# Gaps of 64 bytes between the parts of an SBUF arena, in a chunked-attention, MLP and Strassen mixture kernel

## The chip, the cores and the metric

The kernel runs on one core of a Trainium2 chip. The metric is the device time of one execution in microseconds (us), the median of several runs.

## What is computed

The reference chains three pieces. Its inputs are float32.

```python
# attention within chunks of 64 positions: q, k, v are (4, 8, 576, 64)
scores = scale * matmul(q_c, k_c.T);  attn = exp(scores - max);  attn /= attn.sum + 1e-9
x = (attn @ v_c), heads side by side                       # 2304 x 512
# MLP: w_in 512 x 2048, w_out 2048 x 512
h = maximum(x @ w_in, 0);  x = h * h @ w_out
# mixture of 4 experts, w1 512 x 1024, w2 1024 x 512 each
p = domain_probs / (domain_probs.sum(-1) + 1e-9)
out = sum over e of p[:, e] * (maximum(x @ w1[e], 0) @ w2[e])
```

## The kernel before

Every large product is done three times in float32r: both operands are split into a high and a low part (ACT copies the high part, DVE or POOL subtract it), and high x high, high x low and low x high are summed in PSUM. So a product of a weight tile with a moving tile is three matmuls, each with its own load of 128 x 128 weights. A load runs on the second track of TensorE (PEld in the profile) beside the matmul before it.

All float32r operands but one stand in one SBUF tile, the **arena** `ar` (128 partitions x 128 KiB). Its parts are cut out by hand, by offsets in float32 elements, and it is used twice with two layouts:

- Attention and MLP. `x`, high and low, in five blocks of 384 or 512 tokens (`new_x`); a ring of converted MLP weights (`RING_AT`, `unit_split`); two pairs of buffers for the squared hidden layer (`GP_AT`, in `l1`). `l1` (matmul at L300) multiplies weights from the ring by a block of `x`, `l2` (L333) weights from the ring by a hidden buffer. Each does 12 matmuls, then the other takes its turn.
- Mixture. Seven slots of combined inputs `Y` (`y_slot`), two sets of hidden parts (`S_AT`), two slots of first-layer weights (`W1_AT`, high and low side by side), and one slot of second-layer weights (`W2_AT`); the other second-layer slot is a tile of its own, `w2x`. The loop over `n` (48 steps: 3 super-blocks of tokens x 4 experts x 4 pairs of hidden tiles) has seven units `u`. In each, `c_unit` (L596) does 6 matmuls of 384 columns, with weights from `W1_AT[n % 2]` and one `Y` slot as the moving operand: the first layer as a Strassen-like product of seven. Between these blocks stand second-layer matmuls of the step before: `plain_unit` for steps 0 to 10 (L708, blocks of 6 with 512 columns) and `d_unit` for steps 11 to 47 (L691, blocks of 9 with 256 columns, again seven products). There the hidden parts `g` are the weights, and the split second-layer weights the moving operand: from `W2_AT` where `n` is even, from `w2x` where `n` is odd.

The order on each engine is written out by hand (`tc.manual_schedule()`), with tables for the second layer. DMAs go through SP's queue. During the first 20 ticks attention is interleaved: per tick `s1_stage` has DVE take a maximum (`mx`, L241) and subtract it (L242) twice, and `norm_stage` on DVE sums (`sm`, L253), adds, inverts and scales the tile before. `mx` and `sm` are small tiles, two buffers each.

In front of the change every part of the arena starts at a multiple of 512 bytes from the arena's start, and each 128-column slice of float32 is 512 bytes long. So weights and moving operand, where both are in the arena, stand a multiple of 512 bytes apart. `w2x` starts 155,840 bytes behind the arena's start, which is 304 x 512 + 192.

Of the kernel before, what the change touches and what calls it, by code (L numbers as in the profile page):

```python
# [10 lines left out]
F32 = mybir.dt.float32  # L11
# [7 lines left out]
P = 128  # L19
CH = 64  # L20
BLOCKS = [384, 384, 512, 512, 512]
# [9 lines left out]
RAW_BUFS = 4  # L31
CV_BUFS = 4
HALF = 384
NSUP = 3
LAG_A = 2
UOFF = [1, 3, 5, 16, 8, 17, 18, 19]
# [10 lines left out]
def tile_kernel(ctx, tc, q, k, v, moe_w_in, moe_w_out, moe2_p, moe2_w1, moe2_w2, out):  # L47
    nc = tc.nc
    B, H, S, D = q.shape
# [3 lines left out]
    KD = DM // P  # L53
    HX = H // 2
# [6 lines left out]
    NB = len(BLOCKS)  # L61
    starts = [sum(BLOCKS[:i]) for i in range(NB)]
# [13 lines left out]
    qkp = att.enter_context(tc.tile_pool(name="qkp", bufs=2, side="right"))  # L76
# [1 line left out]


    XW = 2 * KD * NT  # L80
    RING_AT = XW
    GP_AT = RING_AT + RING * 4 * DM
    AR = GP_AT + (LAG + 1) * 2 * 512
    ar = arena.tile([P, AR], F32R, name="ar")


    NY, NW, NS7 = 14 * 2 * HALF, 7 * 2 * P, 14 * HALF
    Y_AT = 0
    S_AT = [NY, NY + NS7]
    W1_AT = [GP_AT - 2 * NW, NY + 2 * NS7]  # L90
    W2_AT = [W1_AT[1] + 2 * NW, GP_AT]
    assert W2_AT[0] + NW <= W1_AT[0] and W2_AT[1] + NW <= AR
    assert W1_AT[0] >= RING_AT + (RING - 2) * 4 * DM

# [3 lines left out]
    def bank(tags):  # L98
        n = turn.get(tags, 0)
        turn[tags] = n + 1  # L100
        tag = tags[n % len(tags)]
        return ps.tile([P, 512], F32, tag=tag, name="ps" + tag, bufs=BUFS[tag])
# [46 lines left out]
    def unit_split(n, which):  # L149
        a = cv.pop((n, which))  # L150
        o = RING_AT + (n % RING * 4 + 2 * which) * DM
        h, l = ar[:, o:o + DM], ar[:, o + DM:o + 2 * DM]
# [14 lines left out]
    qT, kT, et, aT = {}, {}, {}, {}  # L167

    def new_x(tb):
        o, w = 2 * KD * starts[tb], KD * BLOCKS[tb]  # L170
        xh[tb] = ar[:, o:o + w].rearrange("p (k t) -> p k t", k=KD)
        xl[tb] = ar[:, o + w:o + 2 * w].rearrange("p (k t) -> p k t", k=KD)

# [53 lines left out]
    def s1_stage(t, tags):  # L227
        qt, kt = qT.pop(t), kT.pop(t)
        pt = [bank(tags)[:, :HX * CH].rearrange("p (j k) -> p j k", j=HX) for _ in range(2)]
        for c in range(2):  # L230
            cs = slice(c * CH, (c + 1) * CH)
            for j in range(HX):
                for x in range(2):
                    r = slice(x * CH, (x + 1) * CH)
                    nc.tensor.matmul(  # L235
                        pt[x][cs, j, :], lhsT=qt[r, j, cs], rhs=kt[r, j, cs], start=True, stop=True
                    )
        e = qkp.tile([P, HX, 2, CH], F32, tag="e", name="e", bufs=LAG_A + 1)
        mx = qkp.tile([P, 2, HX, 1], F32, tag="mx", name="mx")
        for x in range(2):  # L240
            nc.vector.tensor_reduce(out=mx[:, x], in_=pt[x], axis=AX.X, op=ALU.max)  # L241
            nc.vector.tensor_tensor(  # L242
                out=e[:, :, x, :], in0=pt[x], in1=mx[:, x].to_broadcast([P, HX, CH]), op=ALU.subtract
            )
        et[t] = e
# [3 lines left out]

    def norm_stage(t):  # L250
        e = et[t].rearrange("p j x k -> p (j x) k")
        sm = qkp.tile([P, H, 1], F32, tag="sm", name="sm")
        nc.vector.tensor_reduce(out=sm, in_=e, axis=AX.X, op=ALU.add)  # L253
        nc.vector.tensor_scalar_add(sm, sm, 1e-9)
        nc.vector.reciprocal(sm, sm)
        nc.vector.tensor_tensor(out=e, in0=e, in1=sm.to_broadcast([P, H, CH]), op=ALU.mult)
# [106 lines left out]
    NP = nf2 // 2  # L363
    NQ = NSUP * E * NP
    rows = {}
    for sp in range(NSUP):
        if sp < NSUP - 1:
            r = [starts[2 * sp] + i * P for i in range(3)] + [starts[2 * sp + 1] + i * P for i in range(3)]
        else:
            r = [starts[NB - 1] + i * P for i in range(3)] + [starts[2 + i] + HALF for i in range(3)]  # L370
        rows[sp] = r
# [4 lines left out]
    comb = {}  # L376

    def y_slot(i):
        o = Y_AT + i * 4 * HALF
        return [ar[:, o + z * 2 * HALF:o + (z + 1) * 2 * HALF].rearrange("p (k t) -> p k t", k=2) for z in range(2)]  # L380

    def y_half(a, k):
        return a[:, 2 * k:2 * k + 2, :HALF]

# [3 lines left out]
    def y_blocks(sp):  # L388
        if sp < NSUP - 1:
            return acc[2 * sp], acc[2 * sp + 1]  # L390
        return acc[NB - 1], acc[0]

    def y_combine(sp):

        a, b = y_blocks(sp)
        y11, y21, y12, y22 = y_half(a, 0), y_half(a, 1), y_half(b, 0), y_half(b, 1)
        c = comb[sp] = {Y11: y11, Y21: y21, Y22: y22}
        if sp == 0:
            t1, t2, t3, t4 = y11, y22, y12, y21
        else:  # L400
            u, w = (acc[0], acc[1]) if sp == 1 else (acc[1], acc[2])
            t1, t2, t3, t4 = y_half(u, 0), y_half(u, 1), y_half(w, 0), y_half(w, 1)
        if sp == 0:
            for i in (Y11, Y21, Y22):
                yield from y_split(sp, i)
        sub(t1, y12, y11)
        yield
        sub(t3, y22, y12)
        yield
        sub(t2, y22, t1)  # L410
        yield
        sub(t4, y21, t2)
        c.update({T1: t1, T2: t2, T3: t3, T4: t4})
        yield
        if sp == 0:
            for i in (T1, T2, T3, T4):
                yield from y_split(sp, i)

    def y_split(sp, i):
        h, l = y_slot(i)  # L420
        a = comb[sp][i]
        nc.scalar.copy(h, a)
        eng = nc.vector if sp == 0 or i in (Y11, Y21, Y22) else nc.gpsimd
        eng.tensor_tensor(out=l, in0=a, in1=h.bitcast(F32), op=ALU.subtract)
        yield

    def y_gather():

        for i in range(3):
            nc.gpsimd.tensor_scalar(  # L430
                out=acc[0][:, :, i * P:(i + 1) * P], in0=acc[2 + i][:, :, HALF:], scalar1=1.0,
                scalar2=None, op0=ALU.mult,
            )
            yield
# [73 lines left out]
    def w1_slot(n):  # L508
        o = W1_AT[n % 2]
        w1c[n] = ar[:, o:o + NW], ar[:, o + NW:o + 2 * NW]  # L510
        return ar[:, o:o + 2 * NW].bitcast(F32)
# [36 lines left out]

    def w2_split(n, part):
        if part == 0:  # L550
            o = S_AT[n % 2] + 8 * HALF
            w2c[n] = [ar[:, o + z * 2 * DM:o + (z + 1) * 2 * DM].rearrange("p (h d) -> p h d", h=2) for z in range(2)]
        h, l = (y[:, part] for y in w2c[n])
        a = raw2[n][:, part]
        nc.scalar.copy(h, a)
        nc.gpsimd.tensor_tensor(out=l, in0=a, in1=h.bitcast(F32), op=ALU.subtract)
# [22 lines left out]
    def c_unit(n, u):  # L579
        ws, ys = UNITS[u]  # L580
        if u == 0:
            st[n, "b"] = bank("t")
            o = S_AT[n % 2]
            g[n] = [
                [ar[:, o + (2 * i + z) * HALF:o + (2 * i + z + 1) * HALF] for z in range(2)] for i in range(7)
            ]
        elif u == 1:
            st[n, "c"] = bank("h")
        elif u == 3:
            st[n, "d"] = bank("t")  # L590
        p = st[n, "bcbdbdb"[u]][:, :HALF]
        wh, wl = (y.rearrange("p (s k f) -> p s k f", s=7, k=2)[:, ws] for y in w1c[n])
        yh, yl = y_slot(ys)
        for kk in range(2):
            for z, (w, y) in enumerate(((wh, yh), (wh, yl), (wl, yh))):
                nc.tensor.matmul(  # L596
                    p, lhsT=w[:, kk, :], rhs=y[:, kk, :],
                    start=(kk == 0 and z == 0 and u in (0, 1, 3)),
                    stop=(kk == 1 and z == 2 and u in (1, 5, 6)),
                    skip_group_check=True,  # L600
                )
# [251 lines left out]
    with tc.manual_schedule():  # L853
# [44 lines left out]
        def run(chunks, n=None):  # L898
            while n is None or n > 0:
                try:  # L900
                    next(chunks)
                except StopIteration:
                    return
                n = None if n is None else n - 1
# [25 lines left out]
        for r in range(LEAD + NS + LAG):  # L930
# [12 lines left out]
            if r < NTILE + LAG_A:  # L943
                if r < NTILE:
                    s1_stage(r, tags)
                if 0 <= r - 1 < NTILE:
                    norm_stage(r - 1)
# [47 lines left out]
        for n in range(NQ + 2):  # L995
            sp, m = divmod(n, NU)
            if m == 2 and n < NQ:
                pend["y"] = y_gather() if sp == 1 else iter(())
            if m == 6 and sp + 1 < NSUP:
                pend["y"] = y_combine(sp + 1)  # L1000
            for u in range(7):
# [57 lines left out]
                for back in (0, 1):  # L1059
                    s1, m1 = divmod(n - back, NU)  # L1060
                    if n >= back and m1 == NU - 1 and s1 + 1 < NSUP and u + 7 * back in SPLITS:
                        run(y_split(s1 + 1, SPLITS[u + 7 * back]))
# [25 lines left out]
```

## Time and profile before

| | |
|---|---|
| median of 3 runs (lowest, highest) | 1225.62 us (1225.17, 1226.4) |
| the profiled execution: its own time, its span | 1226.38 us, 1224.5 us |
| instructions in the profile | 21,396 |
| matmuls, weight loads | 8047 each |
| mean granted TensorE clock | 0.993 |
| HBM read, written | 189.30 MB, 63.44 MB |

The time of an execution is its span, from the first to the last instruction, and 1.9 us around it. Of the 8047 matmul records 6663 are float32r matmuls on the arena; the rest belong to attention's transposes and 64 x 64 products and to a short warm-up.

### The profile page before, as it was taken

What the parts mean: (1) busy time and instruction counts of PE and PEld (TensorE: products, weight loads), DVE (VectorE), ACT (ScalarE), POOL (GpSimd) and SP (SyncE); (2) the same over time, 40 slices, a digit from 0 to 9 for tenths busy, and PEclk for the clock granted to TensorE, in tenths of its full rate; (3) what the DMA queues carried; (4) which work ended last, traced back from release to release, by engine and by line L of the source; (5) the groups of instructions that cost most, each with busy time, mean ns of one, the idle gap of its engine ahead of it and who ended that gap; (6) DMA issues with size and microseconds to landing.
All of it is one profiled execution on the core that took longest, in us unless ns stands there. A gap on an engine that the chain in (4) does not pass through costs nothing.

```text
span 1224.5 us, 21396 instructions
## 1 busy us (share of the span) xinstructions
PE 1196.7 (98%) x8047; PEld 1111.0 (91%) x8047; DVE 826.0 (67%) x1379; ACT 602.7 (49%) x1221; POOL 714.7 (58%) x686
## 2 busy tenths in 40 slices
PE   7899999999999999999999999999999999999997
PEld 5798888889888988888988999999999999999996
DVE  6975667656747466455555777676767776767676
ACT  5654555534534345644442556454445654545453
POOL 3410057726745455777881667667756766566665
PEclk8999999999999999999999999999999999999999
DMA  9855023552453644577767668666666686666652
GB/s 212 191 115 155 20 86 119 184 189 86 172 199 102 207 155 151 212 257 256 267 232 300 260 253 297 266 252 256 245 248 258 246 293 241 241 241 249 248 227 112
DMA packets 136230, 254.12 MB, mean 208 GB/s; under 512 B 64960, under 2 KB 110016, under 8 KB 129984
## 3 DMA queue, kind: packets, MB, share of 16 engines
q1 hardware_dynamic: 133504, 252.12, 59.1%
q8 instruction: 63, 1.03, 0.3%
q10 hardware_dynamic: 2624, 0.66, 0.3%
q14 instruction: 39, 0.32, 0.1%
HBM read 189.30 MB, written 63.44 MB: 206 GB/s over the span
## 4 chain that ended last, share of the span: by engine, by line
PE 89%; DVE 6%; ACT 1%; DMA 1%; issue 1%; POOL 1%; SPq 0%; DVEq 0%; ACTq 0%; POOLq 0%
PE pst L596 23%; PE psa L691 21%; PE psa L333 15%; PE pst L300 9%; PE psa L708 8%; PE psh L300 6%; PE psh L596 4%; PE pst L276 1%; PE pst L220 1%; PE pst L235 1%; DMA v<-in_v 1%; PE pst L262 1%; DVE o L791 1%; DVE uw L747 1%; DVE o L790 0%
## 5 line engine op out<-in xcount | busy, mean ns | idle before, releaser
L596 PE MATMUL pst<-ar 128*128 128x384 f32 x1728 | 345.6, 336 | 2.0 <-DVE psh L636 1.7
L596 PEld LDWEIGHTS pst<-ar 128*128 128x128 f32 x1728 | 293.7, 188 | 7.7 <-DVE psh L636 2.0
L333 PE MATMUL psa<-ar 128*128 128x512 f32 (+1 forms) x960 | 219.4, 372 | 1.2 <-ACT ar L316 0.4
L333 PEld LDWEIGHTS psa<-ar 128*128 128x128 f32 x960 | 173.5, 188 | 27.4 <-DVE ar L317 2.0
L622 POOL TENSOR_TENSOR ar<-s,ar 128x384 fp32r<-128x384 f32 x148 | 151.3, 1034 | 68.9 <-ACT ar L621 67.4
L691 PE MATMUL psa<-w2x,ar 128*128 128x256 f32 x1197 | 160.1, 278 | 2.5 <-DVE uw L745 2.3
L691 PE MATMUL psa<-ar 128*128 128x256 f32 x1134 | 158.0, 283 | 1.8 <-DVE uw L741 0.7
L691 PEld LDWEIGHTS psa<-w2x,ar 128*128 128x128 f32 x1197 | 154.8, 188 | 4.2 <-DVE uw L745 2.5
L691 PEld LDWEIGHTS psa<-ar 128*128 128x128 f32 x1134 | 151.2, 188 | 4.1 <-DVE uw L747 1.9
L145 POOL TENSOR_TENSOR raw<-raw 128x512 f32<-128x512 f32 x32 | 34.4, 1073 | 180.4 <-DVE raw L144 73.3
L759 POOL TENSOR_TENSOR o<-o,x 128x256 f32<-128x256 f32 x104 | 82.7, 795 | 80.3 <-ACT x L755 78.0
L300 PE MATMUL pst<-ar 128*128 128x512 f32 (+1 forms) x576 | 127.2, 369 | 0.0
L300 PEld LDWEIGHTS pst<-ar 128*128 128x128 f32 x576 | 105.4, 188 | 14.3
L629 ACT COPY u<-pst 128x384 f32<-128x384 f32 x144 | 69.7, 484 | 94.3 <-PE pst L596 92.2
L640 ACT ACTIVATE ar<-psh 128x384 fp32r<-128x384 f32 x96 | 47.3, 493 | 137.9 <-DVE psh L636 74.6
L621 ACT CAST ar<-s 128x384 fp32r<-128x384 f32 x148 | 75.8, 513 | 73.0 <-DVE s L617 67.9
L708 PE MATMUL psa<-ar 128*128 128x512 f32 x396 | 102.5, 394 | 0.0
L747 DVE TENSOR_TENSOR uw<-psa,uw 128x512 f32<-128x512 f32 x111 | 73.3, 687 | 34.6 <-PE psa L691 21.2
L300 PE MATMUL psh<-ar 128*128 128x512 f32 (+1 forms) x384 | 89.7, 376 | 2.2 <-DVE ar L284 2.2
L708 PEld LDWEIGHTS psa<-ar 128*128 128x128 f32 x396 | 73.2, 188 | 11.7 <-DVE ar L611 0.3
L745 DVE TENSOR_TENSOR uw<-psa,uw 128x512 f32<-128x512 f32 x81 | 56.0, 691 | 40.1 <-PE psa L691 39.8
L300 PEld LDWEIGHTS psh<-ar 128*128 128x128 f32 x384 | 69.0, 190 | 10.8 <-DVE ar L284 2.3
(136 smaller groups left out, 1936.0 us busy)
## 6 DMA issues: line engine op xcount, KB each, us to landing
ar<-w1d SPq DMA_DIRECT2D x37, 1792.0 KB, 7.3
w2x<-w2d SPq DMA_DIRECT2D x38, 896.0 KB, 7.6
ar<-w2d SPq DMA_DIRECT2D x36, 896.0 KB, 8.1
w2d<-jsplit SPq DMA_DIRECT2D x64, 448.0 KB, 3.5
w1d<-ar SPq DMA_DIRECT2D x11, 1792.0 KB, 8.7
w1d<-ar SPq DMA_DIRECT2D x10, 896.0 KB, 6.1
raw<-in_moe_w_in SPq DMA_DIRECT2D x16, 512.0 KB, 4.5
raw<-in_moe_w_out SPq DMA_DIRECT2D x16, 512.0 KB, 5.0
```

What stands on the lines that cost most here:

```text
L300: nc.tensor.matmul(ph[:, :T], lhsT=w[:, kk, :], rhs=x[tb][:, kk, :], start=(kk == 0 and n == 0), stop=(kk == KD - 1 and n == 2),)
L333: nc.tensor.matmul(o, lhsT=w, rhs=y, start=(f == 0 and n == 0), stop=(f == G - 1 and n == 2))
L596: nc.tensor.matmul(p, lhsT=w[:, kk, :], rhs=y[:, kk, :], start=(kk == 0 and z == 0 and u in (0, 1, 3)), stop=(kk == 1 and z == 2 and u in ...
L621: nc.scalar.copy(h, st[n, nm])
L622: nc.gpsimd.tensor_tensor(out=l, in0=st[n, nm], in1=h.bitcast(F32), op=ALU.subtract)
L629: nc.scalar.copy(s, d if at == 3 else b)
L640: nc.scalar.activation(out=g[n][i][0], in_=c, func=AF.Relu)
L691: nc.tensor.matmul(p, lhsT=w, rhs=y, start=(k in (1, 7) and z == 0), stop=(k in (3, 4) and z == 2), skip_group_check=True,)
L708: nc.tensor.matmul(p, lhsT=w[:, ts], rhs=y[:, i, :], start=(i == 0 and z == 0), stop=(i == 1 and z == 2))
L745: nc.vector.tensor_tensor(out=uw, in0=b, in1=uw, op=ALU.add)
L747: nc.vector.tensor_tensor(out=uw, in0=pb[n, t, 0], in1=uw, op=ALU.add)
L759: nc.gpsimd.tensor_tensor(out=o1[:, :2 * P], in0=o1[:, :2 * P], in1=x, op=ALU.add)
```

## The change

It puts 16 float32 elements (64 bytes) between parts of the arena: between the blocks of `x`, between the slots of `Y`, and between pairs of hidden parts. The parts behind these gaps move. The arena grows by 1 KiB per partition. To make room, `mx` and `sm` now share one buffer.

```diff
+PAD = 16
-    RING_AT = XW
+    RING_AT = XW + (NB - 1) * PAD
-    NY, NW, NS7 = 14 * 2 * HALF, 7 * 2 * P, 14 * HALF
+    NY, NW, NS7 = 14 * 2 * HALF + 6 * PAD, 7 * 2 * P, 14 * HALF + 3 * PAD
-    W1_AT = [GP_AT - 2 * NW, NY + 2 * NS7]
+    W1_0 = GP_AT - 2 * NW - 4 * PAD
+    W1_AT = [W1_0, NY + 2 * NS7]
...
     def new_x(tb):
-        o, w = 2 * KD * starts[tb], KD * BLOCKS[tb]
+        o, w = 2 * KD * starts[tb] + tb * PAD, KD * BLOCKS[tb]
...
-        mx = qkp.tile([P, 2, HX, 1], F32, tag="mx", name="mx")
+        mx = qkp.tile([P, 2, HX, 1], F32, tag="mx", name="mx", bufs=1)
...
-        sm = qkp.tile([P, H, 1], F32, tag="sm", name="sm")
+        sm = qkp.tile([P, H, 1], F32, tag="mx", name="sm", bufs=1)
...
     def y_slot(i):
-        o = Y_AT + i * 4 * HALF
+        o = Y_AT + i * (4 * HALF + PAD)
...
         if part == 0:
-            o = S_AT[n % 2] + 8 * HALF
+            o = S_AT[n % 2] + 8 * HALF + PAD
...
             g[n] = [
-                [ar[:, o + (2 * i + z) * HALF:o + (2 * i + z + 1) * HALF] for z in range(2)] for i in range(7)
+                [
+                    ar[:, o + i // 2 * PAD + (2 * i + z) * HALF:o + i // 2 * PAD + (2 * i + z + 1) * HALF]
+                    for z in range(2)
+                ]
+                for i in range(7)
             ]
```

From these offsets follows how far the weights of a matmul stand behind its moving operand, in bytes modulo 512 (called its distance from here on; lines of the kernel before). The three matmuls of a product have the same distance, and so have the 12 of a call of `l1` or `l2` and the 6 of a call of `c_unit`.

| matmuls | before | after |
|---|---|---|
| L300, 960 | 0 | 256, 192, 128, 64, 0 for the five blocks of `x`, 192 each |
| L333, 960 | 0 | 0 |
| L596, 2016 | 0 | 64 and 320: 144 each; 0, 128, 192, 256, 384 and 448: 288 each |
| L708, 396 | 0 | 448: 198; 0: 198 |
| L691, `n` even, 1134 | 0 | 128, 192 and 256: 324 each; 320: 162 |
| L691, `n` odd (`w2x`), 1197 | 320 | 384, 448 and 0: 342 each; 64: 171 |

No engine's instructions change their order or number. On DVE one thing is added, in attention. Its rows around the second `norm_stage` (`pst`, `psh` are PSUM tiles, `cv` and `raw` those of the conversion of MLP weights; DVE_49 is DVE's own semaphore), before:

```order
L241 TENSOR_REDUCE mx<-pst 128x4 [waits PE_49]
L242 TENSOR_TENSOR e<-pst,mx 128x4x64 [waits DVE_49]
L241 TENSOR_REDUCE mx<-psh 128x4 [waits PE_49]
L242 TENSOR_TENSOR e<-psh,mx 128x4x64 [waits DVE_49]
L253 TENSOR_REDUCE sm<-e 128x8 [waits Activation_49]
L254 TENSOR_SCALAR sm<-sm 128x8 [waits DVE_49]
```

and in the change:

```order
L243 TENSOR_REDUCE mx<-pst 128x4 [waits PE_49]
L244 TENSOR_TENSOR e<-pst,mx 128x4x64 [waits DVE_49]
L243 TENSOR_REDUCE mx<-psh 128x4 [waits PE_49]
L244 TENSOR_TENSOR e<-psh,mx 128x4x64 [waits DVE_49]
L255 TENSOR_REDUCE sm<-e 128x8 [waits DVE_49,Activation_49]
L256 TENSOR_SCALAR sm<-sm 128x8 [waits DVE_49]
```

The sum now also waits for DVE's instruction just before it, since it writes over `mx`. That is so in 17 of the 18 calls of `norm_stage`.

## Rows read from the trace of the kernel before

**Rows 1.** The page: busy time by engine, and the granted clock in 40 slices.
```profile
PE 1196.7 (98%) x8047; PEld 1111.0 (91%) x8047; DVE 826.0 (67%) x1379; ACT 602.7 (49%) x1221; POOL 714.7 (58%) x686
...
PEclk8999999999999999999999999999999999999999
```

**Rows 2.** Busy time by stretch (columns named in the first line): attention, MLP, L708's, L691's.
```profile
core 0: us, PE busy (x) PEld busy (x) DVE busy (x) ACT busy (x) POOL busy (x), PEclk, DMA share, GB/s
0.00:151.00 151.00, 136.08 (x1633) 117.14 (x1634) 107.17 (x225) 83.47 (x155) 32.53 (x32) 0.95 0.62 140
151.00:473.00 322.00, 320.76 (x1592) 279.55 (x1591) 202.91 (x312) 146.00 (x272) 187.09 (x176) 1.00 0.44 146
473.00:730.00 257.00, 254.91 (x1381) 233.09 (x1380) 153.96 (x246) 121.89 (x235) 170.92 (x150) 1.00 0.69 253
730.00:1224.50 494.50, 484.99 (x3446) 481.19 (x3444) 361.96 (x600) 251.29 (x559) 324.19 (x330) 1.00 0.65 244
```

**Rows 3.** The page: the chain that ended last, by engine.
```profile
PE 89%; DVE 6%; ACT 1%; DMA 1%; issue 1%; POOL 1%; SPq 0%; DVEq 0%; ACTq 0%; POOLq 0%
```

**Rows 4.** Who waited for whom on PE, three rows of 16.
```profile
PE pst L220 <- DMA q<-in_q: 2.9, 2, 1.7
PE psa L691 <- DVE uw L745: 2.7, 2, 2.3
...
PE pst L220 <- DVE e L242: 1.4, 1, 1.4
```

**Rows 5.** Groups by shape on PE: line, op, out<-in, shapes, count | busy us, mean ns.
```profile
L596 PE MATMUL pst<-ar 128*128 128x384 f32 x1728 | 345.6, 336 | 2.0 <-DVE psh L636 1.7 <-ACT u L629 0.4
L691 PE MATMUL psa<-w2x,ar 128*128 128x256 f32 x1197 | 160.1, 278 | 2.5 <-DVE uw L745 2.3 <-DVE uw L747 0.2
L691 PE MATMUL psa<-ar 128*128 128x256 f32 x1134 | 158.0, 283 | 1.8 <-DVE uw L741 0.7 <-DVE uw L745 0.4 <-DVE uw L747 0.3
L333 PE MATMUL psa<-ar 128*128 128x512 f32 x576 | 141.3, 391 | 0.0
...
L300 PE MATMUL pst<-ar 128*128 128x512 f32 x360 | 86.7, 390 | 0.0
```

**Rows 6.** PE in order of time (start us, us), a step with odd `n`.
```profile
1034.82 1.21 PE L596 MATMUL pst<-ar 128*128 128x384 f32 x6
1035.86 1.18 PE L691 MATMUL psa<-w2x,ar 128*128 128x256 f32 x9
1036.88 1.21 PE L596 MATMUL pst<-ar 128*128 128x384 f32 x6
```

**Rows 7.** The same, a step with even `n`.
```profile
1051.63 1.21 PE L596 MATMUL pst<-ar 128*128 128x384 f32 x6
1052.68 1.23 PE L691 MATMUL psa<-ar 128*128 128x256 f32 x9
1053.74 1.21 PE L596 MATMUL pst<-ar 128*128 128x384 f32 x6
```

**Rows 8.** The same, in the MLP.
```profile
384.44 2.88 PE L300 MATMUL psh<-ar 128*128 128x512 f32 x12
387.16 2.88 PE L333 MATMUL psa<-ar 128*128 128x512 f32 x12
```

**Rows 9.** The same, where L708 takes turns with L596.
```profile
507.36 1.55 PE L708 MATMUL psa<-ar 128*128 128x512 f32 x6
508.75 1.21 PE L596 MATMUL pst<-ar 128*128 128x384 f32 x6
```

**Rows 10.** DVE in order of time, around the second `norm_stage`.
```profile
19.35 0.41 DVE L241 TENSOR_REDUCE mx<-psh 128x4 f32<-128x256 f32 x1
19.80 0.42 DVE L242 TENSOR_TENSOR e<-psh,mx 128x256 f32<-128x256 f32 x1
20.14 0.68 DVE L253 TENSOR_REDUCE sm<-e 128x8 f32<-128x512 f32 x1
```

## The prediction

> **What bounds the kernel now.** The busy times come first: PE is busy for 98% of the span, no other engine for more than 67%, and the granted clock is in the topmost tenth (its 2.4 GHz level) in all slices but the first [rows 1]. By stretch, PE is busy 320.76 us of 322 in the MLP, 254.91 of 257 while L708 runs and 484.99 of 494.5 while L691 runs; only attention's 151 us leave it 15 us idle [rows 2]. The chain that ended last goes through PE for 89% [rows 3]. So in three of four stretches the time is the sum of the starts of one matmul after another, and it can only change if a matmul takes longer or shorter. No instruction is added on PE or taken away. What is left to look at is the pace of single matmuls.
>
> A record's length contains a pipeline tail that overlaps with the next one, so the pace is better read from starts. Twelve matmuls of 512 columns take 387.16 − 384.44 = 2.72 us, 226.7 ns each [rows 8]. Six of 384 columns take 1.04 us, 173.3 ns each, and nine of 256 columns with the moving operand in `w2x` 1.02 us, 113.3 ns each [rows 6]. Nine of 256 columns with both operands in the arena take 1.06 us, 117.8 ns each [rows 7].
>
> The first two differ by 53.4 ns for 128 columns, which is 0.417 ns per column, one column per clock of 2.4 GHz. At that rate 512 columns are 213.3 ns, 384 are 160.0 and 256 are 106.7. Over this the matmuls lose 13.3, 13.3 and 11.1 ns where both operands are in the arena, whatever they compute, and 6.7 ns with `w2x`. The lengths by group tell the same: 283 ns for the arena, 278 for `w2x`, both with 256 columns [rows 5]. **The one class of matmuls at a distance other than 0, namely 320, is 5 ns faster than its twins at distance 0.** The weights of both classes come from the arena, and the work around them is the same.
>
> **The change part by part.** *Distances.* By the table of the change, 768 matmuls of L300 leave distance 0, 1728 of L596, 198 of L708 and 1134 of L691; 342 of L691 (odd `n`) come to it. L333's 960 stay there. That is 768 + 1728 + 198 + 1134 − 342 = 3486 net. The trace shows one price, for distance 320 against 0: 5 ns. For 64, 128, 192, 256, 384 and 448 it shows none. The bounds: at best such a matmul loses its whole 13.3 ns, at worst it loses more than now. How much more, the nearest row tells: L708's blocks of six, which stand between blocks of another width, take 508.75 − 507.36 = 1.39 us, 231.7 ns each [rows 9], against 226.7 for the same 512 columns in undisturbed runs of twelve [rows 8]. So the loss at distance 0 already varies by 5 ns with what went before, and I take −5 to +13.3 ns as the ends. I choose +5 ns, because it is the only difference between distances that was measured, and use it for all widths: 3486 × 5 ns = **17.4 us** less. All of it lies on PE's path.
>
> The Trainium skill speaks against this gain. "TensorE: Matmul & The Clock Gate", section "Step-by-step: what each phase is for", says that the matmul's streaming and the loading of weights have independent SBUF read ports, so that a load takes no bandwidth from the running matmul; by it the sum would be 0. The 283 and 278 ns do not fit it well, as the two groups differ in nothing but where the moving operand stands.
>
> *The shared buffer of `mx` and `sm`.* L242 starts at 19.80 us and ends at 20.22; L253 starts at 20.14, 0.08 us before that end. L242, which does wait for DVE's instruction before it, starts at 19.80, 0.04 us after the end at 19.76 [rows 10]. So the added wait costs 0.08 + 0.04 = 0.12 us, 17 times: 2.0 us on DVE. I count it as nothing on the path. DVE is busy 107 of attention's 151 us [rows 2], and PE waited for L242's result once, for 1.4 us [rows 4]. Without that cover it would be 2.0 us later. Behind the waiting sum stand the rest of `norm_stage` and the conversion of MLP weights; the second is next to be late.
>
> *Transfers.* The kept weights lie elsewhere in the arena, with the same sizes and the same issues. They were hidden, since the DMA that PE waited for longest was attention's `q`, 2.9 us in all [rows 4]. I count nothing.
>
> *Who may stop the gain.* If PE is 17 us quicker, the other engines have 3% less time where L691 runs. DVE is busy there for 362 us of 494.5, POOL for 324, the DMA engines for 65% [rows 2], and PE's longest wait there was 2.3 us [rows 4]. None becomes the bound.
>
> **Sum.** 1226.4 us of the profiled execution − 17.4 = 1209.0. That execution stands 0.8 us above the median shown, so for a median: **1208.2 us**.
>
> **The rivals.**
>
> *Every second distance.* The loss may repeat not every 512 bytes but every 128: then distances 128, 256 and 384 are as bad as 0, and only odd multiples of 64 help. For it: 320 is one of these. Against it: nothing in the trace. Leaving distance 0 for an odd multiple are 384 of L300, 864 of L596, 198 of L708 and 162 + 324 = 486 of the even `n` of L691, while 342 + 342 of the odd `n` go from 320 to an even multiple: 384 + 864 + 198 + 486 − 684 = 1248. Times 5 ns: 6.2 us, 1219.4 us.
>
> *Distance does nothing.* What sets `w2x` apart may be that it is another tile, far from the arena, and the 13.3 ns may be the price of changing weights beside any stream. For it: the loss is 13.3 ns for 384 and 512 columns alike, in the MLP and in the mixture, as a fixed price would be. Against it: the price is not fixed for `w2x`. Then 1225.6 us, or up to 2 us more if DVE's waits show. By the ports of the Trainium skill's page, named above, this is the case to expect. The trace agrees only so far as two groups of equal loss go.
>
> *Slower: the streams never settle.* Weights and moving data are read at the same time, and each change of distance from one unit to the next may throw the two out of the rhythm that they reach at a constant distance. Such a change now comes with every call of `c_unit` and between `l1` and `l2`. Its price is the 5 ns of L708's disturbed blocks: 3486 × 5 ns = 17.4 us more, 1243 us; if half of the changed matmuls are hit, 8.7 us, 1234.3. It decides if the mean loss over the distances is above today's 13.3 ns. For it: [rows 9]. Against it: the blocks that alternate between distances 0 and 320 in [rows 6] are the faster ones.
>
> **How the numbers follow.** Two tenths of a per cent, 2.5 us, is about what a measurement of this kernel can tell from no change. I give my forecast (most distances help) 0.38, every second distance 0.15, no effect 0.20, slower 0.27. So faster is 0.53, the same 0.20, slower 0.27. The likeliest case's own range is 3 to 9 ns per matmul, 1195 to 1215 us. The range must also take in the other cases: I let it reach from 1195 to 1238. The upper end is 3.5 ns more per changed matmul. Outside are a gain nearer to 13.3 ns (0.07) and the full price of the slower rival (0.11).
>
> **What would show it.** If I am right, L691's two groups and L596's, by shape, are shorter by some 5 ns in the mean, L333's keeps its 391 ns, and L300 gains except in its last block. If L596's mean stays at 336 and only L691's two groups move toward each other, distance does nothing general. If blocks of L596 become uneven with the `Y` slot, some distances help and others hurt, and their mix sets the sign. I am wrong altogether if PE's waits, not its pace, change.

## The result, and the profile after

The changed kernel takes 1234.16 us (median of 3, 1232.73 to 1235.31) against 1225.62 before: 1.0068 of before, with an interval of 1.0045 to 1.0091. It is slower by 8 us. The forecast was 17.4 us faster, and the sign was wrong; the time lies within the stated range.

The profiled execution has a span of 1232.4 us, 7.9 us more. Its page, busy time by engine and the chain by engine:

```profile
PE 1203.8 (98%) x8047; PEld 1115.9 (91%) x8047; DVE 827.3 (67%) x1379; ACT 603.1 (49%) x1221; POOL 715.8 (58%) x686
...
PE 89%; DVE 6%; issue 1%; ACT 1%; DMA 1%; POOL 1%; SPq 0%; DVEq 0%; ACTq 0%; POOLq 0%
```

PE's busy time has grown by 7.1 us with the same 8047 matmuls, beside [rows 1]; the chain has not changed, beside [rows 3]. So it is the pace of single matmuls that has changed. The groups by shape on PE (count, then busy us and mean ns; L596 is now L602, L691 is L697, L333 L335, L708 L714, L300 L302):

```profile
L602 PE MATMUL pst<-ar 128*128 128x384 f32 x1728 | 347.1, 337 | 2.0 <-DVE psh L642 1.7 <-ACT u L635 0.4
L697 PE MATMUL psa<-w2x,ar 128*128 128x256 f32 x1197 | 165.5, 283 | 2.7 <-DVE uw L751 2.3 <-DVE uw L753 0.4
L697 PE MATMUL psa<-ar 128*128 128x256 f32 x1134 | 157.5, 282 | 1.9 <-DVE uw L747 0.6 <-DVE uw L753 0.5 <-DVE uw L751 0.4
L335 PE MATMUL psa<-ar 128*128 128x512 f32 x576 | 141.6, 392 | 0.0
L714 PE MATMUL psa<-ar 128*128 128x512 f32 x396 | 101.9, 392 | 0.0
L302 PE MATMUL pst<-ar 128*128 128x512 f32 x360 | 87.9, 392 | 0.0
...
L302 PE MATMUL psh<-ar 128*128 128x512 f32 x216 | 55.2, 398 | 0.0
```

Set against [rows 5] (and, for the rows that [rows 5] leaves out, against the same view of before):

```profile
L708 PE MATMUL psa<-ar 128*128 128x512 f32 x396 | 102.5, 394 | 0.0
...
L300 PE MATMUL psh<-ar 128*128 128x512 f32 x216 | 54.4, 395 | 0.0
```

The `w2x` group, the quick one before, went from 278 to 283 ns, and its busy time from 160.1 to 165.5 us, 5.4 us more. The other half of L691 went from 283 to 282 ns, 0.5 us less. L596's large group rose by 1 ns and 1.5 us; the MLP's three 512-column groups by 1, 2 and 3 ns (0.3 + 1.2 + 0.8 us); L708 fell by 2 ns and 0.6 us. That is 5.4 − 0.5 + 1.5 + 2.3 − 0.6 = 8.1 us; the other groups together took 1.0 us less, which leaves PE's 7.1. More than five of them are a loss of what the kernel before already had, and nowhere did distances other than 0 bring the forecast 5 ns.

In time order, an L302 block at distance 128 (the third block of `x`) and the same block of the kernel before, at distance 0, both between L333's blocks of 384 columns:

```profile
225.88 2.96 PE L302 MATMUL pst<-ar 128*128 128x512 f32 x12
228.68 2.25 PE L335 MATMUL psa<-ar 128*128 128x384 f32 x12
```

```profile
224.90 2.92 PE L300 MATMUL pst<-ar 128*128 128x512 f32 x12
227.66 2.27 PE L333 MATMUL psa<-ar 128*128 128x384 f32 x12
```

From start to start that is 2.80 us against 2.76: 233.3 ns a matmul instead of 230.0.

### The profile page after: what moved, and what is told of

Same layout as the page of the kernel before. It is cut to its first block, busy times and chain, and to the rows that moved or that the text cites. A ratio compares the mean times of both kernels' runs of the same rounds, so it can differ in the third digit from the quotient of the medians.

```text
span 1232.4 us, 21401 instructions
## 1 busy us (share of the span) xinstructions
PE 1203.8 (98%) x8047; PEld 1115.9 (91%) x8047; DVE 827.3 (67%) x1379; ACT 603.1 (49%) x1221; POOL 715.8 (58%) x686
## 4 chain that ended last, share of the span: by engine, by line
PE 89%; DVE 6%; issue 1%; ACT 1%; DMA 1%; POOL 1%; SPq 0%; DVEq 0%; ACTq 0%; POOLq 0%
PE pst L602 23%; PE psa L697 21%; PE psa L335 15%; PE pst L302 9%; PE psa L714 7%; PE psh L302 6%; PE psh L602 4%; PE pst L278 1%; PE pst L237 1%; PE pst L222 1%; DMA v<-in_v 1%; PE pst L264 1%; DVE uw L753 1%; DVE o L796 0%; DVE o L797 0%
## 5 line engine op out<-in xcount | busy, mean ns | idle before, releaser
L602 PE MATMUL pst<-ar 128*128 128x384 f32 x1728 | 347.1, 337 | 2.0 <-DVE psh L642 1.7
L602 PEld LDWEIGHTS pst<-ar 128*128 128x128 f32 x1728 | 294.2, 188 | 7.3 <-DVE psh L642 2.0
L335 PE MATMUL psa<-ar 128*128 128x512 f32 (+1 forms) x960 | 219.7, 372 | 1.2 <-DVE ar L319 0.3
L335 PEld LDWEIGHTS psa<-ar 128*128 128x128 f32 x960 | 173.6, 188 | 28.0 <-DVE ar L319 2.0
L697 PE MATMUL psa<-w2x,ar 128*128 128x256 f32 x1197 | 165.5, 283 | 2.7 <-DVE uw L751 2.3
L697 PEld LDWEIGHTS psa<-w2x,ar 128*128 128x128 f32 x1197 | 159.6, 188 | 4.5 <-DVE uw L751 2.5
L697 PE MATMUL psa<-ar 128*128 128x256 f32 x1134 | 157.5, 282 | 1.9 <-DVE uw L747 0.6
L697 PEld LDWEIGHTS psa<-ar 128*128 128x128 f32 x1134 | 150.9, 188 | 4.5 <-DVE uw L753 2.1
L302 PE MATMUL pst<-ar 128*128 128x512 f32 (+1 forms) x576 | 128.3, 371 | 0.0
L302 PEld LDWEIGHTS pst<-ar 128*128 128x128 f32 x576 | 105.3, 188 | 15.3
L714 PE MATMUL psa<-ar 128*128 128x512 f32 x396 | 101.9, 392 | 0.0
L302 PE MATMUL psh<-ar 128*128 128x512 f32 (+1 forms) x384 | 90.5, 378 | 1.8 <-DVE ar L286 1.8
L714 PEld LDWEIGHTS psa<-ar 128*128 128x128 f32 x396 | 73.3, 188 | 11.5 <-DVE ar L617 0.3
L302 PEld LDWEIGHTS psh<-ar 128*128 128x128 f32 x384 | 69.0, 190 | 11.0 <-DVE ar L286 1.9
```

The lines of the kernel that those rows point to most:

```text
L302: nc.tensor.matmul(ph[:, :T], lhsT=w[:, kk, :], rhs=x[tb][:, kk, :], start=(kk == 0 and n == 0), stop=(kk == KD - 1 and n == 2),)
L335: nc.tensor.matmul(o, lhsT=w, rhs=y, start=(f == 0 and n == 0), stop=(f == G - 1 and n == 2))
L602: nc.tensor.matmul(p, lhsT=w[:, kk, :], rhs=y[:, kk, :], start=(kk == 0 and z == 0 and u in (0, 1, 3)), stop=(kk == 1 and z == 2 and u in ...
L697: nc.tensor.matmul(p, lhsT=w, rhs=y, start=(k in (1, 7) and z == 0), stop=(k in (3, 4) and z == 2), skip_group_check=True,)
L714: nc.tensor.matmul(p, lhsT=w[:, ts], rhs=y[:, i, :], start=(i == 0 and z == 0), stop=(i == 1 and z == 2))
```

## The experiments

After the result the theories were these. **Theory 1:** the distance modulo 512 sets the pace, and 320 happens to be good, most others not. **Theory 2:** `w2x` was quick since it is another tile, far away, and distance is nothing. **Theory 3:** distance is nothing, but a change of it from block to block costs. Ratios below are to runs of the kernel before on the same chip (medians of 1226.23 to 1226.62 us), with 95% intervals. The three kernels without the computation were executed once each.

### The pace by itself

`pace` has no computation in it: after loading a tile `near` and a tile `far` with data, it runs

```python
for cols in (256, 384, 512):
    for d in range(0, 512, 32):
        block(f"c{cols}d{d}b", 20, 8192 + d // 4, near, cols)   # 20 matmuls, weights at 8192 + d // 4
...
```

> Left out: the whole computation; this kernel only times matmuls. Blocks of 20 float32r matmuls, each with its own weight load, at one constant distance per block: c256, c384 and c512 with all distances in steps of 32 bytes and both operands in one tile (moving operand fixed, weights moved), f256 to f512 with the moving operand in a far tile, m384 with the weights fixed and the moving operand moved. Theory 1, the distance modulo 512 sets the pace: c256d0b 283 ns mean and c256d320b 278, f the same as c at equal distance, m384 the same as c384; c512 at 64 and 128 above c512 at 0 by 5 to 9 ns. Theory 2, the far tile is what was fast and distance is nothing: all c groups of one width equal within 1 ns, f groups 5 ns below them. Theory 3, only a change of distance costs: inside blocks of one constant distance all groups of a width equal, c and f alike.

Groups by shape on PE (the name tells width and distance; then busy us and mean ns of one), for 256 columns, some in the far tile:

```profile
L75 PE MATMUL c256d0b<-near 128*128 128x256 f32 x20 | 2.6, 283 | 0.0
...
L75 PE MATMUL c256d64b<-near 128*128 128x256 f32 x20 | 2.5, 281 | 0.0
...
L75 PE MATMUL c256d192b<-near 128*128 128x256 f32 x20 | 2.4, 276 | 0.0
...
L75 PE MATMUL c256d256b<-near 128*128 128x256 f32 x20 | 2.6, 283 | 0.0
...
L75 PE MATMUL c256d320b<-near 128*128 128x256 f32 x20 | 2.5, 281 | 0.0
...
L75 PE MATMUL c256d448b<-near 128*128 128x256 f32 x20 | 2.4, 276 | 0.0
...
L75 PE MATMUL f256d0b<-far,near 128*128 128x256 f32 x20 | 2.6, 283 | 0.0
...
L75 PE MATMUL f256d192b<-far,near 128*128 128x256 f32 x20 | 2.5, 279 | 0.0
```

and for 512 columns:

```profile
L75 PE MATMUL c512d0b<-near 128*128 128x512 f32 x20 | 4.7, 391 | 0.0
...
L75 PE MATMUL c512d64b<-near 128*128 128x512 f32 x20 | 4.8, 396 | 0.0
...
L75 PE MATMUL c512d128b<-near 128*128 128x512 f32 x20 | 4.8, 395 | 0.0
...
L75 PE MATMUL c512d192b<-near 128*128 128x512 f32 x20 | 4.8, 392 | 0.0
...
L75 PE MATMUL c512d256b<-near 128*128 128x512 f32 x20 | 4.7, 389 | 0.0
```

Distance matters, so theories 2 and 3 fall as whole explanations: at distance 0 the far tile gives the same 283 ns as the near one. But three things differ from theory 1. Distances 256 apart give equal means, to within 2 ns where the first matmuls after a switch still count: **the pattern repeats every 256 bytes, not 512.** **For 512 columns distance 0 (or 256) is the quickest of all**, by 4 to 7 ns against any distance but 192 (1 to 3 ns); for 384 columns the means lie between 335 (distance 0) and 339 (distance 160). Only for 256 columns is 0 (or 256) the slowest. And distance 320 had 281 ns here, not the 278 of `w2x`; one distance, 192, gave 276 with the near tile and 279 with the far one. So the distance alone doesn't settle it.

`pace_turns` looks for the rest: blocks of the mixture's widths take turns, with the weights moved and the moving operands in place.

```python
for a in range(0, 512, 64):
    for b in range(0, 512, 64):
        for _ in range(5):
            block(f"x{a}y{b}m", 6, 8192 + a // 4, near, 384)
            block(f"x{a}y{b}n", 9, 12288 + b // 4, near[:, 4096:], 256)
```

> Left out: the whole computation. Six matmuls of 384 columns at distance a and nine of 256 columns at distance b take turns, five times for each pair (a, b) of multiples of 64. Theory 1: the means of the 256-column groups follow b alone, 283 ns for b = 0 and 278 for b = 320, those of the 384-column groups a alone. Theory 3: pairs with a = b are the fastest, all others some 5 ns slower in both groups. A mixture of both shows as a table whose rows and columns both matter.

```profile
L75 PE MATMUL x128y0n<-near 128*128 128x256 f32 x45 | 6.2, 283 | 0.0
...
L75 PE MATMUL x0y0n<-near 128*128 128x256 f32 x45 | 6.1, 281 | 0.0
...
L75 PE MATMUL x0y320n<-near 128*128 128x256 f32 x45 | 6.1, 281 | 0.0
...
L75 PE MATMUL x64y192n<-near 128*128 128x256 f32 x45 | 6.0, 278 | 0.0
L75 PE MATMUL x128y64n<-near 128*128 128x256 f32 x45 | 6.0, 278 | 0.0
```

Rows and columns both matter: distance 64 gives 278 ns beside a block at 128 and 281 beside one at 0 (its twin 320 in the list). Pairs with equal distances are not the quickest, which is against theory 3: by the starts of the blocks a pair takes 2.10 to 2.12 us at equal distances, and 2.08 at (192, 64). And the pair (0, 320), the distances of the kernel's odd steps, again misses their 278 ns. What it does not copy is where `w2x` itself begins.

`pace_pairs` moves that too: weights of the first block at `wa`, of the second at `wb`, its moving operand at `mb`.

```python
block(f"u{wa}w{wb}m{mb}a", 6, 8192 + wa // 4, near, 384)
block(f"u{wa}w{wb}m{mb}b", 9, 12288 + wb // 4, near[:, 4096 + mb // 4:], 256)
...
block(f"v{wa}w{wb}m{mb}b", 6, 12288 + wb // 4, near[:, 4096 + mb // 4:], 512)
```

> Left out: the whole computation. Blocks of six matmuls of 384 columns take turns with blocks of nine of 256 columns (u) or of six of 512 (v); start of the weights of the first (u/v number), of the second (w) and of the second's moving operand (m) in steps of 64 bytes modulo 256, the first's moving operand at 0. Theory 1 with memory: the pair of distances decides, not each by itself; the pair that the kernel before has in its odd steps (0, 0, m 192: distance 0 beside 64 modulo 256) is among the fastest with the 256-column group near 278 ns, (0, 0, 0) has 283. Rival: each group's length follows its own distance alone.

```profile
L75 PE MATMUL u0w0m0b<-near 128*128 128x256 f32 x36 | 4.9, 281 | 0.0
L75 PE MATMUL u0w0m64b<-near 128*128 128x256 f32 x36 | 4.9, 279 | 0.0
...
L75 PE MATMUL u0w0m192b<-near 128*128 128x256 f32 x36 | 4.7, 276 | 0.0
L75 PE MATMUL v0w0m0b<-near 128*128 128x512 f32 x18 | 4.7, 394 | 0.0
L75 PE MATMUL v0w192m192b<-near 128*128 128x512 f32 x18 | 4.6, 391 | 0.0
```

In time order, for u0w0m0 and for u0w0m192:

```profile
36.23 1.21 PE L75 MATMUL u0w0m0a<-near 128*128 128x384 f32 x6
37.27 1.23 PE L75 MATMUL u0w0m0b<-near 128*128 128x256 f32 x9
38.34 1.21 PE L75 MATMUL u0w0m0a<-near 128*128 128x384 f32 x6
...
81.40 1.21 PE L75 MATMUL u0w0m192a<-near 128*128 128x384 f32 x6
82.45 1.18 PE L75 MATMUL u0w0m192b<-near 128*128 128x256 f32 x9
83.47 1.21 PE L75 MATMUL u0w0m192a<-near 128*128 128x384 f32 x6
```

A pair of blocks takes 2.11 us at (0, 0, 0), and 2.07 at (0, 0, 192): close to the 2.11 of [rows 7] and the 2.06 of [rows 6], without any of the kernel's other work. Of the 64 triples (0, 0, 192) was the quickest, by the starts of the blocks. So `w2x`, which begins 192 bytes past a multiple of 512 and so of 256, stood in the best of the places tried, in steps of 64 bytes, for odd steps, and the change took it away. The change with this place kept was not run. Why starts matter beyond their distance is not settled. The last row pair, with equal distance 0 and both operands moved by 192, shows the same for L708's width.

### In the kernel

Two runs move one operand of L691 alone, the arena's second-layer slot for even steps, and `w2x` for odd ones:

```diff
 even320
-    W2_AT = [W1_AT[1] + 2 * NW, GP_AT]
+    W2_AT = [W1_AT[1] + 2 * NW + 48, GP_AT + 48]
 odd0
-                        late["w2"] = late["b"].tile([P, 2, NW], F32R, name="w2x")
+                        w2x = late["b"].tile([P, 2 * NW + 128], F32R, name="w2x")
+                        late["w2"] = w2x[:, 80:80 + 2 * NW].rearrange("p (z c) -> p z c", z=2)
```

> The kernel before with the second-layer weights of even steps moved by 192 bytes, so that all of L691 is at distance 320, nothing else. Theory 1: L691's group from the arena falls from 283 to 278 ns, 1134 x 5 ns = 5.7 us less, 1219.9 us. Theory 2 (far tile): no change, 1225.6 us. Theory 3 (change of distance costs): no gain, or up to 5 us more, since all steps would alternate between 0 and 320.

> The kernel before with w2x moved by 320 bytes, so that all of L691 is at distance 0, nothing else. Theory 1: L691's w2x group rises from 278 to 283 ns, 1197 x 5 ns = 6.0 us more, 1231.6 us, most of what the change cost. Theory 2: no change, the tile is as far away as it was. Theory 3: a constant distance everywhere, so faster or the same.

`even320` took 1222.64 us, 0.9974 of before (0.9965 to 0.9984); `odd0` 1230.31 us, 1.0033 (1.002 to 1.0046). The arena group of L691 with `even320`, and the `w2x` group with `odd0`:

```profile
L691 PE MATMUL psa<-ar 128*128 128x256 f32 x1134 | 153.8, 279 | 2.5 <-DVE uw L747 1.1 <-DVE uw L741 0.9 <-DVE uw L745 0.4
```

```profile
L691 PE MATMUL psa<-w2x,ar 128*128 128x256 f32 x1197 | 166.1, 284 | 2.3 <-DVE uw L745 2.3
```

So 4 ns were gained and 6 ns lost by moving one operand by a few hundred bytes: the forecast's price of 5 ns is real for this line. By the medians both runs gave some two thirds of the 5.7 and 6.0 us.

The change taken apart: the shared buffer alone, the gaps of `x` with it, the gaps of the mixture without it.

```diff
 mx_only, x_only
+        mx = qkp.tile([P, 2, HX, 1], F32, tag="mx", name="mx", bufs=1)
+        sm = qkp.tile([P, H, 1], F32, tag="mx", name="sm", bufs=1)
 x_only
+    RING_AT = XW + (NB - 1) * PAD
+        o, w = 2 * KD * starts[tb] + tb * PAD, KD * BLOCKS[tb]
+    W1_AT = [GP_AT - 2 * NW - 64, NY + 2 * NS7]
+    W2_AT = [W1_AT[1] + 2 * NW, GP_AT + 64]
 mix_only
+    NY, NW, NS7 = 14 * 2 * HALF + 6 * PAD, 7 * 2 * P, 14 * HALF + 3 * PAD
+    W2_AT = [W1_AT[1] + 2 * NW, GP_AT + 64]
...
```

> The kernel before with mx and sm sharing one buffer, no gaps. Theory 1 (distances are all of it): within 1 us of before, since DVE's 17 waits of 0.12 us are covered. Rival (the waits show): 2 us more, 1.0016 of before.

> The change's gaps between the blocks of x alone (and the shared buffer, for room); the mixture is at the distances of before. Theory 1 with the lengths of the run pace: L300's 384 matmuls of 512 columns at distances 64 and 128 take 5 ns more (396 and 395 against 391), its 384 of 384 columns at 192 and 256 the same: 1.9 us more, 1.0016 of before. If the change's loss came from L300 alone: 8 us more.

> The change's gaps in the mixture alone; attention and MLP as before. Theory 1: the w2x group goes from 278 to 283 ns (1197 x 5 = 6.0 us), the arena group of L691 from 283 to 282 (1.1 us less), L596 some 0.5 ns more (1.0 us): 5 to 6 us more in all, 1.0045 of before, and with x_only the whole of the change's 1.0068. If the parts act on each other, the two do not add up to it.

| kernel | median us | ratio to before |
|---|---|---|
| mx_only | 1227.28 | 1.0005 (0.9996 to 1.0014) |
| x_only | 1230.04 | 1.0029 (1.002 to 1.0038) |
| mix_only | 1230.01 | 1.0035 (1.0023 to 1.0046) |
| the change | 1234.16 | 1.0068 (1.0045 to 1.0091) |

The two halves add up: 1.0029 + 0.0035 = 1.0064. `mix_only` has the same groups of L691 as the change, within 1 ns:

```profile
L696 PE MATMUL psa<-w2x,ar 128*128 128x256 f32 x1197 | 166.1, 284 | 2.4 <-DVE uw L750 2.3
L696 PE MATMUL psa<-ar 128*128 128x256 f32 x1134 | 157.5, 282 | 1.9 <-DVE uw L746 0.7 <-DVE uw L750 0.4 <-DVE uw L752 0.4
```

`x_only` has the change's groups in the MLP:

```profile
L301 PE MATMUL pst<-ar 128*128 128x512 f32 x360 | 87.9, 392 | 0.0
...
L301 PE MATMUL psh<-ar 128*128 128x512 f32 x216 | 55.2, 398 | 0.0
```

The profiled executions can be cut in three by the starts of PE's matmuls (us): attention up to its last matmul (with the first blocks of the MLP among it), the MLP from there to the first of L596, the mixture from there to the end.

| | attention | MLP | mixture |
|---|---|---|---|
| before | 159.5 | 329.1 | 735.8 |
| the change | 160.2 | 331.1 | 741.1 |
| x_only | 161.0 | 331.1 | 736.3 |
| mix_only | 157.5 | 329.1 | 740.7 |
| odd0 | 159.5 | 329.1 | 741.1 |
| even320 | 157.7 | 329.1 | 733.1 |

The gaps of `x` cost 2.0 us, in the MLP, where 1.9 were expected; the gaps of the mixture 4.9, where 5 to 6 were. Attention's part differs by 1.8 us even between `even320` and the kernel before, which are the same there, so the time of a single execution says little about a cost of 1 or 2 us. The medians of `x_only` and `mix_only`, 3.4 us above before each, lie 1.5 us above and at least 1.6 below what was expected. For `x_only` the granted clock goes with some of it: its 11 executions have a mean of 0.9903 of 2.4 GHz, the 23 of before beside them 0.9918, and at equal clock it is 2.1 to 2.7 us longer (1230.3 against 1227.6 us at 0.990, 1228.8 against 1226.7 at 0.992, 1227.7 against 1225.2 at 0.994). Why its clock is lower is open. The shared buffer is within noise, as expected.

The last three test what the bare paces foretold. `even448` and `even64` replace the 48 of `even320` by 112 and 16 elements, which gives distances 64 and 448. `even320_plain` adds to `even320`:

```diff
-            o = S_AT[n % 2] + 8 * HALF
+            o = S_AT[n % 2] + 8 * HALF + 48
...
-            o = S_AT[n % 2]
+            o = S_AT[n % 2] + 48 * plain(n)
```

> The kernel before with the second-layer weights of even steps moved by 448 bytes: distance 64, which is 320 less 256. Theory, the pattern repeats every 256 bytes: the same as even320, L691's arena group at 279 ns, 0.997 of before. Rival, every 512 bytes: distance 64 is a distance of its own, the group anywhere from 279 to 283 ns, no reason to be equal.

> The kernel before with the second-layer weights of even steps moved by 64 bytes: distance 448. Theory, the pair of blocks decides as in the run pace_pairs: (0, 0, 64) took 2106.7 ns for a pair of blocks and (0, 0, 0) 2113.3, 126 pairs, 0.8 us less, 0.9993 of before; L596's blocks beside it a little longer, L691's a little shorter. Rival, any distance but 0 is quick for 256 columns: 5 us less, as was forecast for the change, 0.996.

> even320 with the hidden parts and the second-layer weights of steps 0 to 10 moved by 192 bytes, so that L708's blocks stand at (0, 192, 192). By pace_pairs these take 2416.5 ns with L596's six against 2433.5 at (0, 0, 0): 66 pairs, 1.1 us less than even320, 0.9965 of before. If only each group's own distance counted, nothing: L708 stays at distance 0.

| kernel | median us | ratio to before |
|---|---|---|
| even448 | 1221.96 | 0.9967 (0.9955 to 0.998) |
| even64 | 1225.04 | 0.9995 (0.9986 to 1.0004) |
| even320_plain | 1220.28 | 0.9957 (0.9944 to 0.9969) |

The arena group of `even448`, then of `even64`, then L708 of `even320_plain`:

```profile
L691 PE MATMUL psa<-ar 128*128 128x256 f32 x1134 | 153.8, 279 | 2.5 <-DVE uw L747 1.1 <-DVE uw L741 0.9 <-DVE uw L745 0.4
```

```profile
L691 PE MATMUL psa<-ar 128*128 128x256 f32 x1134 | 156.7, 281 | 2.0 <-DVE uw L741 0.8 <-DVE uw L745 0.4 <-DVE uw L747 0.3
```

```profile
L708 PE MATMUL psa<-ar 128*128 128x512 f32 x396 | 101.4, 391 | 0.0
```

All three came out as foretold. A move by 256 bytes more gives the same 279 ns, so for this line the period is 256 in the kernel too. A distance other than 0 in the wrong place gains next to nothing (0.9995). And L708's group fell from 394 to 391 ns with its distance still 0, 1.1 us of busy time; the intervals of `even320_plain` and `even320` overlap, so the group shows this, and not the time. `even320_plain` is quicker than the kernel before, 0.9957, and than the change.

## Why the prediction was wrong

**What bounds the kernel** held: the time changed with the pace of PE's matmuls, by the same 7 to 8 us as PE's busy time, and no other engine's wait grew to matter: PE's longest was 2.4 us, for attention's `q`.

**The step that failed is the sum's one price**: "I choose +5 ns, because it is the only difference between distances that was measured, and use it for all widths". The 5 ns were real for 256 columns at one distance and one start. For the other widths they had the wrong sign or none: at 512 columns a block at distance 64 loses 5 ns (396 against 391), and at 384 columns the mean moves between 335 and 339. The 13.3 ns that matmuls lose at distance 0 were lifted by no other distance: for 384 and 512 columns no block of `pace` settled below them, by its matmuls' starts. Of the terms, by busy time, L596's 1728 x 5 = 8.6 us less became 1.5 us more, L300's 768 x 5 = 3.8 us less 2.0 us more, and the 1134 x 5 = 5.7 us less of L691 at even steps 0.5 us less. One of the prediction's own signs came: L596's blocks are uneven with the `Y` slot. Sorted by slot and step in the change's trace, the records at distances 64 and 128 have a mean of 338.8 ns, at 384 of 337.7, and at the other five of 335.6 to 336.0; sorted in the same way, before has 335.2 to 335.9 throughout. Some distances hurt here, and none helped.

The same step missed a loss. "342 of L691 (odd `n`) come to it" counted only those that reach distance 0 as losing. The other 855 odd-step matmuls went to distances 64, 384 and 448, and they lost as well, even more: by product, the records of these three are 4.7 to 6.0 ns longer than the same ones before, those that came to distance 0 2.5 ns. The term of 342 x 5 = 1.7 us more became 5.4 us more for the whole `w2x` group.

**The rivals.** "Distance does nothing" is refuted by `pace`, `even320` and `odd0`. The Trainium skill's page "TensorE: Matmul & The Clock Gate", section "Step-by-step: what each phase is for", says that loading weights takes no read bandwidth from the running matmul, as the two have independent ports. The traces do not agree with what was drawn from it, a pace without regard to place: 396 against 391 ns at 512 columns with nothing changed but where the weights stand, and the measurement decides. That it is the two reads that collide no run shows. "Every second distance" was right that the repeat is shorter than 512, and wrong in the period, 256 rather than 128: 64 and 192 differ. "Slower: the streams never settle" had the right sign, and its case of half the matmuls hit gave 1234.3 us, close to the 1234.16 measured. That closeness is luck, for the mechanism was only half right. A block's pace does depend on the block that takes turns with it, as `pace_turns` shows; yet at constant distance within 20 matmuls 64 and 128 stay slow for 512 columns, and most of the loss is the good place of `w2x` given up.

**The shared buffer** cost nothing on the path, as predicted. DVE in the changed kernel around the second `norm_stage`:

```profile
19.76 0.42 DVE L244 TENSOR_TENSOR e<-psh,mx 128x256 f32<-128x256 f32 x1
20.29 0.69 DVE L255 TENSOR_REDUCE sm<-e 128x8 f32<-128x512 f32 x1
```

The sum now starts 0.53 us after the subtraction's start, instead of 0.34 in [rows 10]: 0.19 us more, where 0.12 was worked out, but covered.

## What to carry to other kernels

In these runs of float32r matmuls with their own weight loads, back to back, the place of weights and moving operand in SBUF was worth some per cent of the pace (113 to 120 ns from start to start at 256 columns in `pace`). Where a kernel has such matmuls, measure this for each width, and for the pair of blocks that take turns, in a bare kernel before spreading one observed difference over all of them. A class that stands out as quick in a profile may be standing at a good place by chance: protect it first, and try its twins there. Here one move of 192 bytes gave 0.3%, and gaps that spread one line over eight distances, and others over up to five, cost 0.7%.

## What the runs showed that was not expected

In blocks of constant distance the pace repeats with the distance modulo 256 bytes. At 512 columns blocks of constant distance lie between 389 and 396 ns in mean length, best at 0 and 256; at 256 columns between 276 and 283, worst at 0 and 256. And the pace depends on more than the distance: 256 columns at distance 64 modulo 256 took 276 ns at (0, 0, 192) and 281 ns in `pace`, and six matmuls of 512 columns at distance 0 took 391 or 394 ns with both operands moved by the same 192 bytes. So where the neighbours vary, the distance modulo 256 doesn't settle the pace: L596's records in the change, sorted as above, have 338.8 ns at distance 64 and 335.6 at 320. What in the chip makes the start and the neighbouring block count is open.
